# Mixture of experts after selective attention: the singles' first layer turned round, and the last scatters and row fetches placed elsewhere

## The chip, the cores and the metric

The kernel runs on one core of a Trainium2 chip. The metric is the device time of one execution in microseconds (us), the median over several. TensorE multiplies matrices and writes its results to PSUM banks of 128 partitions x 512 float32; ScalarE, VectorE and GpSimd work on them and on SBUF; SyncE and GpSimd issue the transfers (DMA).

## The reference, cut to what matters

```python
# q, k, v: (8, 8, 576, 64), s: (8, 8, 576); x = attention output as (8, 576, 512)
logits = x @ w_gate                         # 8 experts
local_gate = sigmoid(x @ w_local)
for b in range(B):
    for s in range(S):                      # an expert is fresh, or kept from the token before
        e = argmax(logits[b, s]) if s == 0 or local_gate[b, s] < 0.5 else prev_e
        prev_e = e
        h = maximum(x[b, s] @ w1[e], 0)     # w1[e]: 512 x 1024
        out[b, s] = softmax(logits[b, s])[e] * (h @ w2[e])   # w2[e]: 1024 x 512
```

All of it is float32. There are 8 x 576 = 4608 tokens of 512 numbers, and each goes through one expert of two layers. The attention ahead of it is causal, with a bias from a cumulative sum of s.

## The kernel before, in words

**Attention and sorting.** The first third of the time, up to about 255 us, is attention, in 32 steps of one batch and two heads each. As batches are done, groups of them are sorted by expert (class `Group`): `rank` gives each token a slot in a table of rows in memory, `rows_d`, in which each expert has a stretch of its own, and `scatter` writes 128 tokens at a time to their slots by an indirect transfer on GpSimd. A row is 586 numbers (2344 bytes): the token, its number and its gate. The last group, batches 6 and 7, is sorted while the experts' stage already runs, and has ten scatters. After its rank, `Sort.tables` computes on VectorE which expert and which row each later unit of work has, and `Sort.fill` closes each expert's stretch with empty rows, by transfers on SyncE's queue.

**Units of the experts' stage** (`experts`). There are 26 units, in a fixed order: two early ones of 256 rows, whose experts are known beforehand, and then the pattern of `ORDER`, "DDMSSDDMSSDDMSSDDMSSDSDS". D is a double, 256 rows of one expert. S is a single, 128 rows of one expert. M is mixed, 64 rows of each of two experts. There are ten singles. For each unit:

- `load`: the expert's weights w1 and w2, 4 MB, on SyncE's queue, into one of four rooms. The fourth lies in `x4`, the tile that held the tokens of four batches; it is handed to `experts` as `w3`. Of it, the columns from `WS` = 8192 on are not used by weights, and hold `hx`.
- `fetch`: 128 rows at a time from `rows_d`, on GpSimd's queue, behind a read of the row's number from the tables.
- `turn_x`: rows to columns, by VectorE's 32x32 block transposes (L1088), 16 instructions for 128 rows; two small copies (L1104, L1105) keep number and gate.
- `layer1`: for doubles and singles the weights are stationary (128x128) and the turned rows move (256 or 128 columns), so that the result has h already with its hidden index on partitions, as layer 2 wants it (L1231, then an activation on ScalarE, L1235). For mixed units it is the reverse: the rows are stationary, 64 of each expert in one half of the array's columns, and 512 columns of weights move (L1214). Their h comes with rows on partitions, is written to `hx` (L1216), and VectorE turns it into `hT` (L1222, 16 instructions).
- `layer2`: h stationary, 512 columns of w2 moving (L1244); ScalarE multiplies by the gate (L1248, `y`); GpSimd scatters 128 output rows to `out` (L1249).

In the loop, the order written for unit i is: weights of later units, `turn_x(i + 2)`, the first half of `layer1(i + 1)`, `fetch(i + 3)`, the other half, `layer2(i)`. On TensorE therefore the first layer of a unit comes one block before the second layer of the unit ahead of it. Each engine runs its own instructions strictly in the order in which the program writes them.

**Hooks and ticks.** The sorting of the last group is woven into the first units. Matmul groups call `tick()`, and `hooks` lists pairs of a step count and a function; when the count is reached the function's instructions are written at that place in the program. Units 0 and 1 have 16 ticks in each first layer, and 8 in each 128 rows of the second. The ten scatters are one hook at tick 16, the tables eight hooks at ticks 18 to 32, and two final checks stand at 60 and 66.

**The start of the stage** is written out by hand:

```python
        layer1(1, 0, FK)
        load(0)
        fetch(2)
        fetch(3)
        for k in range(2):
            layer2(0, k)
        load(1)
        for k in range(2):
            turn_x(2, k)
        second(1)
```

A fetch of unit 2 or later has to wait until all scatters and fills have landed.

Of the kernel before, what the change touches and what calls it, by code (L numbers as in the profile page):

```python
# [10 lines left out]
F32 = mybir.dt.float32  # L11
# [7 lines left out]
P = 128  # L19
B, H, S, DH = 8, 8, 576, 64  # L20
D = H * DH
E, F = 8, 1024
# [8 lines left out]
DK, FK = D // P, F // P  # L31
# [6 lines left out]
WS = DK * F + FK * D  # L38
XW = XI + 2
R = N + 2 * P  # L40
HALF = P // 2
# [25 lines left out]
@with_exitstack  # L67
def kernel(
    ctx: ExitStack,
    tc: tile.TileContext,  # L70
    q: bass.AP,
    k: bass.AP,
    vm: bass.AP,
    vt: bass.AP,
    kz: bass.AP,
    vz: bass.AP,
    vx: bass.AP,
    s: bass.AP,
    w_gate: bass.AP,
    w_local: bass.AP,  # L80
    w1: bass.AP,
    w2: bass.AP,
    out: bass.AP,
):
    nc = tc.nc
    mm, tr = nc.tensor.matmul, nc.tensor.transpose
    cum_d = nc.dram_tensor("cum", (B * H, S), F32, kind="Internal")
    x_d = nc.dram_tensor("x_tokens", (N, D), F32, kind="Internal")
    rows_d = nc.dram_tensor("x_rows", (E * R + 2 * P, XW), F32, kind="Internal")

    ctx.enter_context(tc.manual_schedule(engines=None))
    const = ctx.enter_context(tc.tile_pool(name="const", bufs=1))
    ident = const.tile([P, P], F32, name="ident")
    make_identity(nc, ident)
    lg = const.tile([P, NM, E + 1], F32, name="lg")
    nc.vector.memset(lg, 0.0)
    recs = const.tile([P, NPAIR, 2 * NB], F32, name="recs")
    nc.vector.memset(recs, 1.0)
    out_of = const.tile([P, 2], I32, name="out_of")
    sort = Sort(tc, const, lg, rows_d, ident, TOPS)  # L100

    with ExitStack() as main:
        keep = main.enter_context(tc.tile_pool(name="keep", bufs=1))
        x4 = keep.tile([P, 4 * NB * XW], F32, name="x4")
        xs = {}

        def new_x(b):
            xs[b] = x4[:, b % 4 * NB * XW : (b % 4 + 1) * NB * XW].rearrange("p (t w) -> p t w", w=XW)
            return xs[b]


        plan = {}

        def at(n, half, *what):
            plan.setdefault((n, half), []).extend(what)

        place = 0
        for bs in ((0, 1), (2, 3), (4,), (5,)):
            n = HP * bs[-1] + HP + 1
            g = sort.group(bs, xs)  # L120
            at(n, 2, g.choose, g.codes)
            at(n + 1, 1, g.rows)
            at(n + 1, 2, g.fresh, g.share, g.held)
            at(n + 2, 1, g.hold)
            at(n + 2, 2, g.hot, g.gates)
            at(n + 3, 1, g.count)
            at(n + 3, 2, g.rank)
            for f in g.scatters:
                place = max(place + (2 if n < 17 else 1), 3 * (n + 4))
                at(place // 3, (3, 4, 0)[place % 3], f)  # L130
        at(3, 0, sort.constants)
        at(26, 2, sort.early)
        gx = main.enter_context(tc.tile_pool(name="gx", bufs=5))
        w = keep.tile([P, WS], F32, name="w0")
        ready = {"w": {0: w}, "x": {}}
        for i in range(8):
            at(14 + i, 0, lambda bank, i=i: load_weights(nc, w, w1, w2, EARLY[0], (i,)))

        def fetch_early(bank):
            for i, e in enumerate(EARLY):  # L140
                for k in range(2):
                    ready["x"][i, k] = gx.tile([P, XW], F32, name="xg")
                    r0 = e * R + k * P
                    nc.sync.dma_start(ready["x"][i, k], rows_d[r0 : r0 + P, :])

        at(27, 1, fetch_early)

        fx = main.enter_context(tc.tile_pool(name="fx", bufs=2))
        turned = ready["turned"] = Turned(nc, fx, main.enter_context(tc.tile_pool(name="first", bufs=2)), ident)
        for j in range(8):  # L150
            at((29, 29, 30, 30, 30, 31, 31, 31)[j], 2,
               lambda bank, j=j: turned.squares(0, j // 4, 2, ready["x"][0, j // 4], (j % 4,)))
        at(31, 2, lambda bank: [turned.extras(0, k, ready["x"].pop((0, k))) for k in range(2)])
        last = sort.group((6, 7), xs)

        attention(tc, q, kz, vz, vx, s, w_gate, w_local, ident, lg, recs, const, new_x, plan)
        tables = sort.tables()
        check = in_range(main.enter_context(tc.tile_pool(name="g_sb", bufs=1)), nc, recs, sort.total, sort.ones, out_of)
        hooks = [(2, last.choose), (2, last.codes), (6, last.rows), (6, last.fresh), (6, last.held), (8, last.share),
                 (11, last.hold), (11, last.hot), (13, last.count), (13, last.rank), (15, last.gates),  # L160
                 (16, lambda bank: [f(bank) for f in last.scatters]),
                 *((18 + 2 * i, lambda bank: next(tables, None)) for i in range(8)),
                 *((60 + 6 * i, lambda bank, f=f: f(bank)) for i, f in enumerate(check))]
        experts(tc, w1, w2, out, rows_d, ident, sort, early_units() + units(), hooks, x4, gx, ready)
    def number(x, most):
        return nc.values_load(x[0:1, 0:1], min_val=0, max_val=most, skip_runtime_bounds_check_because="a count")

    ALL = P * NPAIR * 2 * NB
    with tc.If(number(out_of[:, 1:], ALL + MOST[2]) > 0):
        total = number(sort.total, MOST[2])  # L170
        with tc.If(total > SLOTS[2]):
            experts(tc, w1, w2, out, rows_d, ident, sort, units(SLOTS[2], SLOTS[2] + 4))
            with tc.If(total > SLOTS[2] + 4):
                experts(tc, w1, w2, out, rows_d, ident, sort, units(SLOTS[2] + 4, MOST[2]))
        with tc.If(number(out_of, ALL) > 0):
            general(tc, q, k, vm, vt, s, w_gate, w_local, w1, w2, out, cum_d, x_d, rows_d, ident, lg)
# [876 lines left out]
def early_units():  # L1053
    return [("early", i) for i in range(len(EARLY))]
# [54 lines left out]
def experts(ctx, tc, w1, w2, out, rows_d, ident, sort, units, hooks=(), w3=None, gx=None, ready=None):  # L1109
# [7 lines left out]
    mm, tr = nc.tensor.matmul, nc.tensor.transpose  # L1117
    hooks = list(hooks)
# [10 lines left out]
    fp = pool("fp", 2)  # L1129
# [6 lines left out]
    hT, hx = {}, {}  # L1136
# [59 lines left out]
    def layer1(i, first, last):  # L1196

        if i >= NU:
            return
        n = nbs[i] * P  # L1200
        if first == 0:
            hT[i] = fp.tile([P, FK * 2 * P], F32, name="hT")[:, : FK * n].rearrange("p (f n) -> p f n", f=FK)
        w = [ws[s][:, : DK * F].rearrange("p (c f) -> p c f", c=DK) for s in of[i]]
        if len(w) > 1:

            if first == 0:
                hx[i] = w3[:, WS : WS + F] if ready else fp.tile([P, F], F32, name="hx", bufs=1)
            for g in range(first, last, FK // 2):
                ps = ps_h.tile([P, 512], F32, name="hp")
                f = slice(g * P, g * P + 512)  # L1210
                for c in range(DK):
                    for h in range(2):
                        d = slice(h * HALF, h * HALF + HALF)
                        mm(ps[d], lhsT=xT[i][:, c, d], rhs=w[h][:, c, f], start=(c == 0), stop=(c == DK - 1))  # L1214
                    tick()
                nc.scalar.activation(hx[i][:, f], ps, Act.Relu)  # L1216
            if last == FK:
                x = hx.pop(i).rearrange("p (f n) -> p f n", f=FK)
                m = P // 4
                for a in range(0, P, m):  # L1220
                    for d in range(0, P, m):
                        nc.vector.transpose(hT[i][d : d + m, :, a : a + m], x[a : a + m, :, d : d + m])  # L1222
            return
        per = 512 // n
        for g in range(first, last, per):
            ps = ps_h.tile([P, 512], F32, name="hp")
            for j in range(per):
                f = (g + j) * P
                y = ps[:, j * n : j * n + n]
                for c in range(DK):  # L1230
                    mm(y, lhsT=w[0][:, c, f : f + P], rhs=xT[i][:, c, :], start=(c == 0), stop=(c == DK - 1))  # L1231
                for _ in range(nbs[i]):
                    tick()

            nc.scalar.activation(hT[i][:, g : g + per], ps, Act.Relu)  # L1235
# [34 lines left out]
    if ready:  # L1270
# [4 lines left out]

        layer1(1, 0, FK)
        load(0)
        fetch(2)
        fetch(3)
        for k in range(2):  # L1280
            layer2(0, k)
        load(1)
        for k in range(2):
            turn_x(2, k)
# [73 lines left out]
```

## Time and profile before

| | |
|---|---|
| time before | 790.01 us, median of 3 (788.81 to 790.12) |
| span of the profiled execution | 798.9 us |
| TensorE matmuls | 783.0 us, 98% of the span |
| TensorE weight loads (beside matmuls) | 561.8 us |
| VectorE | 338.4 us |
| ScalarE | 237.0 us |
| GpSimd | 175.4 us |
| moved by DMA | 204.47 MB, mean 256 GB/s |

The profile is one execution, with a record for each instruction: start, duration, and what ended the engine's idle time before it. PE is TensorE's matmuls, PEld its weight loads, DVE VectorE, ACT ScalarE, POOL GpSimd, SP SyncE; a name with a q at its end is the engine's queue. A float32 matmul leaves two records. L1231 is line 1231 of the kernel before. Matmuls overlap, and a record's duration is longer than the step from one start to the next, so a block's length is read from its start to the start of the next block. The profiled execution is some 9 us longer than the timed ones.

### The profile page before, as it was taken

What the parts mean: (1) busy time and instruction counts of PE and PEld (TensorE: products, weight loads), DVE (VectorE), ACT (ScalarE), POOL (GpSimd) and SP (SyncE); (2) the same over time, 40 slices, a digit from 0 to 9 for tenths busy, and PEclk for the clock granted to TensorE, in tenths of its full rate; (3) what the DMA queues carried; (4) which work ended last, traced back from release to release, by engine and by line L of the source; (5) the groups of instructions that cost most, each with busy time, mean ns of one, the idle gap of its engine ahead of it and who ended that gap; (6) DMA issues with size and microseconds to landing.
All of it is one profiled execution on the core that took longest, in us unless ns stands there. A gap on an engine that the chain in (4) does not pass through costs nothing.

```text
span 798.9 us, 18230 instructions
## 1 busy us (share of the span) xinstructions
PE 783.0 (98%) x7078; PEld 561.8 (70%) x7078; DVE 338.4 (42%) x1228; ACT 237.0 (30%) x611; POOL 175.4 (22%) x329
## 2 busy tenths in 40 slices
PE   9999999999999989999999999999999999999996
PEld 8989888888888854853777547774577735676762
DVE  3234444454557649325462264522655226546000
ACT  5767766756664111111111111111111111111110
POOL 3422344455432241101210002101111011011001
PEclk9999999999999999999999999999999999999999
DMA  9485579877474389956999369993699946994001
GB/s 312 170 294 186 187 236 303 312 247 237 170 254 179 113 290 411 393 192 242 335 387 408 127 228 352 387 395 116 246 345 394 361 150 229 373 411 188 22 14 43
DMA packets 64145, 204.47 MB, mean 256 GB/s; under 512 B 8269, under 2 KB 8301, under 8 KB 64048
## 3 DMA queue, kind: packets, MB, share of 16 engines
q1 hardware_dynamic: 55008, 172.41, 60.2%
q0 software_dynamic: 8896, 30.47, 10.0%
q8 instruction: 58, 0.95, 0.5%
q14 instruction: 39, 0.32, 0.1%
q10 hardware_dynamic: 144, 0.33, 0.1%
HBM read 179.93 MB, written 23.76 MB: 255 GB/s over the span
## 4 chain that ended last, share of the span: by engine, by line
issue 59%; PE 30%; POOL 4%; DVE 2%; POOLq 1%; SPq 1%; another core or an unknown queue 1%; DMA 0%; DVEq 0%
PE o L408 13%; PE ps L330 11%; POOL out_dram L1249 2%; PE o L370 2%; POOL xg L1184 2%; PE hp L1231 2%; PE o L286 1%; POOLq L1159 1%; PE o L351 1%; SPq L808 1%; PE bank L947 1%; DVE xT L1088 0%; SPq L804 0%; DVE x L413 0%
## 5 line engine op out<-in xcount | busy, mean ns | idle before, releaser
L1088 DVE STREAM_TRANSPOSE xT<-xg 32x128 f32<-32x128 f32 x576 | 174.2, 302 | 173.3 <-PE hp L1231 97.1
L1244 PE MATMUL yp<-w,hT 128*128 128x512 f32 (+1 forms) x528 | 217.6, 595 | 0.0
L1231 PE MATMUL hp<-xT,w 128*128 128x256 f32 (+1 forms) x1088 | 193.0, 337 | 2.8 <-issue 2.5
L1231 PEld LDWEIGHTS hp<-xT,w 128*128 128x128 f32 x1088 | 172.2, 191 | 27.4 <-issue 11.0
L339 ACT ACTIVATE sc<-ps,bias 128x256 f32<-128x256 f32 (+3 forms) x448 | 156.5, 482 | 60.6 <-PE ps L330 58.6
L1244 PEld LDWEIGHTS yp<-w,hT 128*128 128x128 f32 (+1 forms) x528 | 90.7, 181 | 115.4 <-issue 114.5
L1249 POOL DMA_INDIRECT out_dram<-y,at_gate x38 | 38.5, 1012 | 439.9 <-ACT y L1248 425.4
L408 PE MATMUL o<-v,sc 128*64 128x74 f32 x3072 | 117.9, 229 | 3.1 <-issue 2.9
L408 PEld LDWEIGHTS o<-v,sc 128*64 128x64 f32 x3072 | 110.9, 136 | 11.8 <-issue 9.2
L1235 ACT ACTIVATE hT<-hp 128x512 f32<-128x512 f32 x68 | 40.4, 597 | 195.6 <-PE hp L1231 183.3
L1248 ACT ACTIVATE y<-yp,at_gate 128x512 f32<-128x512 f32 x38 | 26.1, 688 | 240.5 <-PE yp L1244 234.3
L345 POOL TENSOR_SCALAR_AFFINE_SELECT sc<-sc 128x256 f32<-128x256 f32 x160 | 66.5, 420 | 129.0 <-ACT sc L339 60.8
L330 PE MATMUL ps<-q,k 64*128 64x320 f32 (+2 forms) x768 | 92.3, 386 | 0.0
L330 PEld LDWEIGHTS ps<-q,k 64*128 64x128 f32 x768 | 69.6, 186 | 14.6 <-ACT r_v L957 0.6
L1244 PE MATMUL yp<-x,hT 128*128 128x512 f32 (+1 forms) x144 | 63.3, 594 | 0.0
L1222 DVE STREAM_TRANSPOSE hT<-x 32x256 f32<-32x256 f32 x64 | 27.9, 436 | 65.4 <-ACT x L1216 64.5
L410 DVE RECIPROCAL recs<-o 128x4 f32<-128x4 f32 x64 | 12.1, 189 | 92.0 <-PE o L408 80.3
L1231 PEld LDWEIGHTS hp<-xT,x 128*128 128x128 f32 x320 | 46.1, 191 | 5.8 <-issue 2.6
L1231 PE MATMUL hp<-xT,x 128*128 128x128 f32 (+1 forms) x320 | 50.1, 317 | 0.0
L1244 PEld LDWEIGHTS yp<-x,hT 128*128 128x128 f32 (+1 forms) x144 | 25.3, 178 | 26.2 <-issue 25.8
L1038 POOL DMA_INDIRECT x_rows<-x,r_slot_i x40 | 38.9, 973 | 9.3 <-issue 5.7
L413 DVE TENSOR_TENSOR x<-o,recs 128x292 f32<-128x292 f32 x64 | 34.5, 538 | 2.2
(163 smaller groups left out, 350.6 us busy)
## 6 DMA issues: line engine op xcount, KB each, us to landing
w<-in_w_dram SPq DMA_DIRECT2D x184, 512.0 KB
x<-in_w_dram SPq DMA_DIRECT2D x56, 512.0 KB
v<-in_vx_dram SPq DMA_DIRECT2D x32, 370.0 KB
vt<-in_vz_dram SPq DMA_DIRECT2D x32, 320.0 KB
k<-in_kz_dram SPq DMA_DIRECT2D x31, 320.0 KB
q<-in_q_dram SPq DMA_DIRECT2D x32, 288.0 KB
xg<-x_rows POOLq DMA_DIRECT2D x30, 293.0 KB
x_rows<-r_empty SPq DMA_DIRECT2D x6, 293.0 KB
```

The costliest lines, as they stand in the source:

```text
L330: mm(ps[:, h, at : at + z - a], lhsT=kb[d, c * P : c * P + P], rhs=qb[d, a:z], start=True, stop=True)
L339: nc.scalar.activation(scs[n, u][:, h, at : at + z - a], raw[u][:, h, at : at + z - a], Act.Exp, bias=bias[:, i : i + 1], scale=scale)
L345: nc.gpsimd.affine_select(out=x, in_=x, compare_op=Alu.is_ge, fill=0.0, base=0, pattern=[[0, 2], [1, P]], channel_multiplier=-1)
L408: mm(y, lhsT=w, rhs=x, start=start, stop=stop)
L413: nc.vector.tensor_tensor(x, y, rec.unsqueeze(3).to_broadcast([P, t1 - t0, 2, HW]), op=Alu.mult)
L1038: self.s.nc.gpsimd.indirect_dma_start(out=next(self.s.views)[:, :], out_offset=bass.IndirectOffsetOnAxis(ap=self.slot[:z, m : m + 1], axis=0),
L1088: self.nc.vector.transpose(self.xT[i][d : d + m, :, k * P + a * m : k * P + a * m + m], rows[a * m : a * m + m, :, X0 + d : X0 + d + m])
L1222: nc.vector.transpose(hT[i][d : d + m, :, a : a + m], x[a : a + m, :, d : d + m])
L1231: mm(y, lhsT=w[0][:, c, f : f + P], rhs=xT[i][:, c, :], start=(c == 0), stop=(c == DK - 1))
L1235: nc.scalar.activation(hT[i][:, g : g + per], ps, Act.Relu)
L1244: mm(ps[n * m : n * m + m, :], lhsT=hT[i][:, c, a : a + m], rhs=wn[:, c, :], start=(c == 0), stop=(c == FK - 1))
L1249: nc.gpsimd.indirect_dma_start(out=next(outs)[:, :], out_offset=bass.IndirectOffsetOnAxis(ap=at[i, k][:, 0:1], axis=0), in_=y[:, :], eleme ...
```

## The change

There are three edits.

1. Singles take the mixed units' way through layer 1: 128 rows stationary, 512 columns of w1 moving, h written to `hx` by ScalarE and turned by VectorE. The condition is now `nbs[i] == 1`, which holds for singles and mixed units; `m` is 128 rows for one expert and 64 for two. `hx` alternates between two places beside the weights. This is for longer matmuls: 8 of 512 columns instead of 32 of 128.
2. The ten scatters of the last group become ten hooks, at ticks 16, 18, ... 34, and the hooks are sorted by tick. This is to spread them over the program.
3. The fetches of units 2 and 3 are written behind the first block of layer 2, so that the rows behind the scatters are read a block later.

```diff
-                 (16, lambda bank: [f(bank) for f in last.scatters]),
+                 *((16 + 2 * i, f) for i, f in enumerate(last.scatters)),
...
+        hooks.sort(key=lambda hook: hook[0])
...
-        if len(w) > 1:
+        if nbs[i] == 1:
             if first == 0:
-                hx[i] = w3[:, WS : WS + F] if ready else fp.tile([P, F], F32, name="hx", bufs=1)
+                at_ = WS + len(hT) % 2 * F
+                hx[i] = w3[:, at_ : at_ + F] if ready else fp.tile([P, F], F32, name="hx", bufs=1)
+            m = P // len(w)
...
-                    for h in range(2):
-                        d = slice(h * HALF, h * HALF + HALF)
-                        mm(ps[d], lhsT=xT[i][:, c, d], rhs=w[h][:, c, f], start=(c == 0), stop=(c == DK - 1))
+                    for h, wh in enumerate(w):
+                        d = slice(h * m, h * m + m)
+                        mm(ps[d], lhsT=xT[i][:, c, d], rhs=wh[:, c, f], start=(c == 0), stop=(c == DK - 1))
...
         layer1(1, 0, FK)
         load(0)
+        layer2(0, 0)
         fetch(2)
         fetch(3)
-        for k in range(2):
-            layer2(0, k)
+        layer2(0, 1)
```

## The prediction

> **What bounds the kernel now.** I read first the page's shares by engine: TensorE has work nearly all the time. Then TensorE's timeline through the expert stage (from 255 us on), because there the question is what separates one block of matmuls from the next.
>
> ```profile
> PE 783.0 (98%) x7078; PEld 561.8 (70%) x7078; DVE 338.4 (42%) x1228; ACT 237.0 (30%) x611; POOL 175.4 (22%) x329
> ...
> 576.04 7.31 PE L1231 MATMUL hp<-xT,w 128*128 128x128 f32 x64
> 583.28 7.09 PE L1244 MATMUL yp<-w,hT 128*64 128x512 f32 x32
> 590.30 7.41 PE L1231 MATMUL hp<-xT,x 128*128 128x128 f32 x64
> 597.55 7.03 PE L1244 MATMUL yp<-w,hT 128*128 128x512 f32 x16
> 604.42 5.78 PE L1231 MATMUL hp<-xT,w 128*128 128x256 f32 x26
> ```
>
> Columns: start, duration, operation, shapes, count. Every block starts just before the former ends; there is no gap to fill. So this stage lasts as long as TensorE's instructions, and only start-to-start times matter. A single's first layer (64 records of 128 columns) takes 583.28 - 576.04 = 7.24 us; its second layer, with the same arithmetic in 16 records of 512 columns, takes 604.42 - 597.55 = 6.87 us. Third, VectorE's and GpSimd's timelines at the same place, for the slack of what must feed TensorE:
>
> ```profile
> 577.26 0.99 POOL L1249 DMA_INDIRECT out_dram<-y,at_gate  x1 [5.86 <-ACT y L1248]
> 578.22 1.18 POOL L1184 DMA_DIRECT2D xg<-x_rows  x2
> ...
> 587.53 5.04 DVE L1088 STREAM_TRANSPOSE xT<-xg 32x128 f32<-32x128 f32 x16 [12.05 <-DMA xg<-x_rows]
> 592.72 5.04 DVE L1088 STREAM_TRANSPOSE xT<-xg 32x128 f32<-32x128 f32 x16
> ```
>
> The rows of the next double are fetched at 578.22, land at 587.53 (9.3 us later) and are turned by 597.8; TensorE wants them at 604.42, so VectorE has 6.6 us to spare here. Last, the beginning of the stage, where the change also works:
>
> ```profile
> 286.00 0.96 POOL L1038 DMA_INDIRECT x_rows<-x,r_slot_i  x1 [0.30 <-DMA x_rows<-r_empty]
> 292.78 1.20 POOL L1184 DMA_DIRECT2D xg<-x_rows  x2 [5.82 <-issue]
> 294.37 1.14 POOL L1184 DMA_DIRECT2D xg<-x_rows  x2 [0.39 <-issue]
> 299.05 1.04 POOL L1249 DMA_INDIRECT out_dram<-y,at_gate  x1 [3.54 <-ACT y L1248]
> ...
> 299.32 5.04 DVE L1088 STREAM_TRANSPOSE xT<-xg 32x128 f32<-32x128 f32 x16 [2.67 <-DMA xg<-x_rows]
> 304.50 5.03 DVE L1088 STREAM_TRANSPOSE xT<-xg 32x128 f32<-32x128 f32 x16
> ...
> 287.08 0.38 PE L1231 MATMUL hp<-xT,w 128*128 128x256 f32 x1 [1.09 <-issue]
> 288.49 0.40 PE L1231 MATMUL hp<-xT,w 128*128 128x256 f32 x1 [1.03 <-issue]
> 289.23 0.77 PE L1231 MATMUL hp<-xT,w 128*128 128x256 f32 x1 [0.34 <-issue]
> 289.79 28.80 PE L1244 MATMUL yp<-w,hT 128*128 128x512 f32 x64
> 318.42 1.89 PE L1231 MATMUL hp<-xT,w 128*128 128x256 f32 x8
> ```
>
> Two things are seen. TensorE limps at 286 to 289.8 (gaps of 1.09 + 1.03 + 0.34 = 2.46 us) while the ten scatters drain, and the four second-layer blocks after it take 318.42 - 289.79 = 28.63 us instead of 4 x 6.87 = 27.48: the hole costs 3.6 us in all. And the rows of unit 2 are turned by 309.5, 8.9 us before TensorE wants them at 318.42.
>
> **What the skill says.** The Trainium skill, "TensorE: Matmul & The Clock Gate", section "Wait — 56ns, not 53.3ns?", gives a warm start-to-start of N / 2.4 GHz plus about 2.5 ns (55.6 ns at N = 128, 215.7 at 512). The trace agrees if a record is two passes: 7.24 us / 64 = 113 ns = 2 x 56.6, and 6.87 / 16 = 429 ns = 2 x 214.7. So what the new form saves is the fixed cost of 48 records, not arithmetic. "SBUF — State Buffer", section "SBUF: two separate sides", says that VectorE takes the port it shares with GpSimd only in a two-port mode or with two SBUF inputs; the transposes have one. The trace agrees: a fetch issued at 592.49, beside transposes, landed in 8.5 us; the one at 578.22, with VectorE idle, in 9.3. "DMA: Bandwidth & Descriptors", section "Anatomy of one DMA — SWDGE (gpsimd) path", has 2.0 us plus bytes / 436e3, an estimate of 2.7 us for 300 KB of rows; the trace shows 6.5 to 9.3 us beside the weights' traffic, and I use the trace.
>
> **Part 1, the singles' first layer.** Ten singles each drop 32 matmuls (64 records) for 8 (16 records of 512 columns). The ten blocks start to start: 7.24, 7.24, 7.24, 7.25, 7.24, 7.25, 7.24, 7.25, 7.15, 7.14, in all 72.24 us. The two at 7.15 have no half-width block beside them; those at 7.24 do, and about 0.09 of that is the change of form, which may stay. New block: 6.87 us, the second layer's. Saving per single between 7.145 - 6.87 = 0.28 and 7.24 - 6.87 = 0.37; ten give 2.8 to 3.5. I take 3.1. The stage is TensorE's, so all of it shortens the end.
>
> Added on VectorE: 16 transposes of 32x256 per single, as the mixed units have (436 ns each, 7.0 us; 7.20 with gaps), 72 us in all on an engine busy 42%. ScalarE's two activations stay two. What waits: h is needed by layer 2 of the same unit, behind layer 2 of the former unit and layer 1 of the next, at least 13.7 us after its own layer 1; 0.7 us of activation and 7.2 of turning fit. Queued behind these transposes on VectorE is the turning of a later unit's rows. The tightest place is a mixed unit, two singles, then a double, four times. With the times above: layer 1 of the first single ends at 582.9, activation to 583.6, h turned 583.6 to 590.9; the double's rows, landed at 587.53, wait 3.4 us and are turned 590.9 to 601.2. TensorE wants them at 604.42 less two savings of 0.31 = 603.8. Slack 2.6 us: hidden. The second single's h follows, 601.2 to 608.4, wanted at 617.6. The weights are no new limit: the last weights load is issued at about 723, and the block that uses it starts at 764.
>
> **Part 2, the ten scatters spread over ticks 16 to 34.** A tick is a place in program order. What stands between the scatters now is TensorE's matmuls, VectorE's tables and SyncE's fills; nothing of it is GpSimd's, and a scatter waits for slots and gates alone, both ready at 273.8. GpSimd will still issue ten in a row (274.5 to 287.0). I cost it at 0, and the 3.6 us hole stays.
>
> **Part 3, the fetch of units 2 and 3 behind the first layer-2 block.** On GpSimd the fetch now stands behind the first output scatter, which waits for ScalarE's y at 298.8 and ends at 300.09. So it issues at 300.1, not 292.78: 7.3 us later. Its landing: bound below 6.5 us (the present one, no output rows ahead), above 9.3 us (the later fetches, behind an output). I take 8.0, as the output's rows here begin to move sooner after their issue: landed 308.1, both turned 10.2 us later (299.32 to 309.5 now), 318.3 plus about 0.1. TensorE wants them at 318.42. The wait is 0 at the lower bound, 1.3 us at the upper; I take 0.4. Unit 3's turning, behind 1.3 us of checks, ends near 330, before 332.46.
>
> Sum: -3.1 + 0 + 0.4 = -2.7. 790.0 - 2.7 = 787.3 us.
>
> **Rivals.** (a) *The late rows bite harder.* They wait as long as the scatters' hole, over 2 us, and TensorE's clock drops as it did there (0.87 and 0.79 granted at 285 to 295). The skill's clock-gate page, "What's actually happening", says that idleness halves the clock for a window of 3.4 us. A second hole of 3.6 us less the saving: 790.0 - 3.1 + 3.6 = 790.5, no difference to be told. For it: 8.9 us of slack shrink to about zero. Against it: the bounds give at most 1.3 us. (b) *VectorE becomes the limit* at mixed, single, single, double. If its 17.5 us of work there ran 25% longer it would be 4.4 us late against 2.6 of slack, 1.8 us at each of four places: 790.0 - 3.1 + 0.4 + 7.2 = 794.5, slower. Against it: the same transposes show 432 to 442 ns in all 64 cases. (c) *The spread does empty the DMA queues* and the 3.6 us hole goes: 787.3 - 3.6 = 783.7. For it: the hole ends when the scatters have landed. Against it: GpSimd's queue.
>
> **Chances and range.** Forecast 0.70, (a) 0.14, (b) 0.08, (c) 0.08. Within the forecast the saving (2.8 to 3.5) and wait (0 to 1.3) give 786.5 to 788.5, nearly all beyond 0.2% (under 788.4). Faster 0.76, same 0.15, slower 0.09. The range must take in (a)'s milder half and part of what leads to (c): 784.8 to 789.8 leaves out about 0.08 on each side.
>
> **What would show it.** Right: singles' first layer as 16 records at 6.9 us from start to start; VectorE near 410 us busy; ten scatters still back to back on GpSimd and TensorE's gaps before 290 still there; the fetch at about 300; the block at 318.4 waiting for VectorE by under 1.3 us; no TensorE wait on h. Wrong: gaps of TensorE before doubles that follow singles, or a gap-free 280 to 290.

## The result, and the profile after

The changed kernel takes 786.21 us (786.01 to 786.34), the kernel before beside it 789.76: ratio 0.9957, 95% interval 0.9939 to 0.9974, so 2.1 to 4.8 us faster. The forecast was 787.3.

TensorE's timeline of the changed kernel, at the place shown of before (start, duration, operation, shapes, count):

```profile
563.41 7.03 PE L1218 MATMUL hp<-w,xT 128*128 128x512 f32 x16
570.37 7.09 PE L1248 MATMUL yp<-w,hT 128*64 128x512 f32 x32
577.38 7.13 PE L1218 MATMUL hp<-x,xT 128*128 128x512 f32 x16
584.36 7.03 PE L1248 MATMUL yp<-w,hT 128*128 128x512 f32 x16
591.22 13.98 PE L1235 MATMUL hp<-xT,w 128*128 128x256 f32 x64
```

The singles' first layers are 16 records now, and last 6.96 and 6.98 us from start to start, instead of 7.24 and 7.25. No gap stands between the blocks. Over the ten singles: 6.96 four times, 6.98 three times, 6.97 once, and 6.87 twice for the two without a half-width block beside them, in all 69.49 us against 72.24 before: 2.75 us less. The page's first part:

```profile
PE 772.8 (98%) x6598; PEld 516.4 (66%) x6598; DVE 407.4 (52%) x1388; ACT 236.9 (30%) x611; POOL 174.5 (22%) x329
```

VectorE rose by 69 us, which is 160 transposes of 436 ns, and none of it appears in the time. VectorE's timeline, and one line of TensorE's, at the tightest kind of place, a double behind two singles:

```profile
481.33 5.04 DVE L1089 STREAM_TRANSPOSE xT<-xg 32x128 f32<-32x128 f32 x16
...
486.52 5.04 DVE L1089 STREAM_TRANSPOSE xT<-xg 32x128 f32<-32x128 f32 x16
...
491.72 7.17 DVE L1226 STREAM_TRANSPOSE hT<-x 32x256 f32<-32x256 f32 x16
498.92 5.05 DVE L1089 STREAM_TRANSPOSE xT<-xg 32x128 f32<-32x128 f32 x16
...
494.23 13.98 PE L1235 MATMUL hp<-xT,w 128*128 128x256 f32 x64
```

No idle time is noted in brackets: VectorE works without a pause. The double's rows are turned at 491.6; TensorE's block that reads them starts at 494.23. Of the 2.6 us of slack forecast, 2.6 are there.

The start of the stage, in TensorE's, GpSimd's and VectorE's timelines:

```profile
263.85 15.75 PE L1235 MATMUL hp<-xT,w 128*128 128x256 f32 x72
279.43 27.63 PE L1248 MATMUL yp<-w,hT 128*128 128x512 f32 x64
306.90 1.89 PE L1235 MATMUL hp<-xT,w 128*128 128x256 f32 x8
...
267.46 0.93 POOL L1039 DMA_INDIRECT x_rows<-x,r_slot_i  x1 [0.38 <-POOL x L1033]
...
278.76 0.96 POOL L1039 DMA_INDIRECT x_rows<-x,r_slot_i  x1 [0.30 <-issue]
287.52 1.00 POOL L1253 DMA_INDIRECT out_dram<-y,at_gate  x1 [7.80 <-ACT y L1252]
289.20 1.20 POOL L1185 DMA_DIRECT2D xg<-x_rows  x2 [0.68 <-DMA w<-in_w_dram]
...
296.17 5.04 DVE L1089 STREAM_TRANSPOSE xT<-xg 32x128 f32<-32x128 f32 x16 [12.40 <-DMA xg<-x_rows]
301.36 5.03 DVE L1089 STREAM_TRANSPOSE xT<-xg 32x128 f32<-32x128 f32 x16
```

GpSimd still issues the ten scatters in a row, from 267.46 to 278.76, which is 11.3 us from the first start to the last; in the profile before it took 11.5 us (274.51 to 286.00). The ticks have spread them over the program's text and not over time.

The hole ahead of the second layer is gone here, and the rows of unit 2 are turned at 306.4, 0.5 us before they are wanted. It is tempting to book the missing hole as a gain of the spread scatters. The span of this profile is 784.5 us against 798.9 before, 14 us less, where the times differ by 3.5. So the two profiles are not of like executions, and the first experiment is a second profile of the kernel before.

### The profile page after: what moved, and what is told of

Read it like the earlier page. It is cut to its first block, busy times and chain, and to the rows that moved or that the text cites. A ratio compares the mean times of both kernels' runs of the same rounds, so it can differ in the third digit from the quotient of the medians.

```text
span 784.5 us, 17433 instructions
## 1 busy us (share of the span) xinstructions
PE 772.8 (98%) x6598; PEld 516.4 (66%) x6598; DVE 407.4 (52%) x1388; ACT 236.9 (30%) x611; POOL 174.5 (22%) x329
## 4 chain that ended last, share of the span: by engine, by line
issue 55%; PE 34%; POOL 4%; DMA 3%; POOLq 1%; DVE 1%; SPq 0%
PE o L409 14%; PE ps L331 12%; PE hp L1235 4%; PE o L371 2%; POOL out_dram L1253 2%; DMA x<-in_w_dram 2%; POOL xg L1185 2%; DMA w<-in_w_dram 1%; POOLq L1160 1%; PE o L352 1%; DMA s_sb<-in_s_dram 1%; DVE xT L1089 1%; PE bank L948 1%; SPq L1051 0%; PE bank L973 0%
## 5 line engine op out<-in xcount | busy, mean ns | idle before, releaser
L1226 DVE STREAM_TRANSPOSE hT<-x 32x256 f32<-32x256 f32 x224 | 97.6, 436 | 133.1 <-ACT x L1220 130.2
L1235 PE MATMUL hp<-xT,w 128*128 128x256 f32 x640 | 140.7, 379 | 0.3 <-DVE xT L1089 0.3
L1235 PEld LDWEIGHTS hp<-xT,w 128*128 128x128 f32 x640 | 121.1, 190 | 20.2 <-issue 3.8
L409 PE MATMUL o<-v,sc 128*64 128x74 f32 x3072 | 113.6, 229 | 0.7 <-issue 0.7
L409 PEld LDWEIGHTS o<-v,sc 128*64 128x64 f32 x3072 | 108.8, 136 | 8.1 <-issue 6.1
L1218 PE MATMUL hp<-w,xT 128*128 128x512 f32 (+1 forms) x208 | 77.8, 595 | 0.0
L1239 ACT ACTIVATE hT<-hp 128x512 f32<-128x512 f32 x48 | 28.6, 597 | 133.0 <-PE hp L1235 133.0
L1218 PEld LDWEIGHTS hp<-w,xT 128*128 128x128 f32 (+1 forms) x208 | 29.8, 165 | 46.5 <-issue 46.5
L1220 ACT ACTIVATE x<-hp 128x512 f32<-128x512 f32 x28 | 16.7, 597 | 78.8 <-PE hp L1218 78.8
```

Source lines behind the costliest of these rows:

```text
L409: mm(y, lhsT=w, rhs=x, start=start, stop=stop)
L1218: mm(ps[d], lhsT=xT[i][:, c, d], rhs=wh[:, c, f], start=(c == 0), stop=(c == DK - 1))
```

## The experiments

They ran in three sets: e1 to e4 on chip 9, then e5 to e8 on chip 12, then e9 and e10 on chip 9 again. Each ratio is to the kernel before in the same set.

**e1, the kernel before once more.** No edit.

> The kernel before, unchanged, for a second profile of it. Theory A: the hole of TensorE at 286 to 290 us in the first profile (3.6 us) and the 7 us that this profile needed longer for attention than the profile after are of that one execution; a second profile has a span near 788.5, the experts' stage begins near 248, and no hole. Rival B: the hole belongs to the kernel before, and is there again at 3 to 4 us. Ratio to before: 1.000 in both.

Ratio 0.9995 (0.9983 to 1.0007), span 786.7. TensorE's and GpSimd's timelines of this second profile of before:

```profile
263.17 15.74 PE L1231 MATMUL hp<-xT,w 128*128 128x256 f32 x72
278.75 27.63 PE L1244 MATMUL yp<-w,hT 128*128 128x512 f32 x64
306.21 1.89 PE L1231 MATMUL hp<-xT,w 128*128 128x256 f32 x8
...
287.07 1.20 POOL L1184 DMA_DIRECT2D xg<-x_rows  x2 [8.03 <-DMA w<-in_w_dram]
288.68 1.13 POOL L1184 DMA_DIRECT2D xg<-x_rows  x2 [0.40 <-issue]
290.11 1.04 POOL L1249 DMA_INDIRECT out_dram<-y,at_gate  x1 [0.30 <-issue]
```

No hole. This execution took 788.3 us, so those that gave 789.8 us can hardly have had one either. And edit 3 is seen for what it does in this set: in the kernel before the fetch waits until 287.07, and the first output, ready at about 286.6, stands behind it until 290.11; in the changed kernel the output goes at 287.52 and the fetch at 289.20. Counted from the start of the second layer, the fetch comes 1.5 us later (9.77 against 8.32), not 7.3.

**e2, edit 1 alone.** The changed kernel with edits 2 and 3 taken back.

```diff
-                 *((16 + 2 * i, f) for i, f in enumerate(last.scatters)),
+                 (16, lambda bank: [f(bank) for f in last.scatters]),
...
-        layer2(0, 0)
         fetch(2)
         fetch(3)
-        layer2(0, 1)
+        for k in range(2):
+            layer2(0, k)
```

> Edit 1 alone; scatters and fetches as before. Theory A: all of the gain is here: the ten first layers lose 2.75 us (72.24 to 69.49), so the ratio is 0.9965, 787.0 against 789.8, and whatever of the measured 3.55 lies beyond that is the measurement's spread. Rival B: placing the scatters and fetches brought 0.8 us or more: then this kernel stands 0.8 us above the changed kernel in the same call.

785.59 us, ratio 0.9956 (0.9943 to 0.9970). That is the whole change's ratio, 0.9957. All of the gain is edit 1. From the start of unit 2's first layer to the end of the profile, e1 takes 786.7 - 306.21 = 480.5 us and e2 783.3 - 305.64 = 477.7: 2.8 us, the 2.75 counted block by block. The timed gain of 3.5 us does not contradict this: 2.75 us is a ratio of 0.9965, inside both intervals. A few tenths more than 2.75 may be real, and no line of the profile shows them.

**e3, edits 2 and 3 alone.** The kernel before with the two other parts of the change's diff.

> Edits 2 and 3 without edit 1. Theory A: GpSimd issues the scatters in a row as before, and the rows of unit 2 are turned just in time: ratio 1.000, within 0.3 us. Rival B: ratio 0.9985 or less (1.2 us or more faster), with the hole before 290 us gone. Rival C: the late rows cost: TensorE waits 0.5 to 1.3 us ahead of unit 2's first layer, ratio 1.0006 to 1.0016.

788.83 us, ratio 1.0003 (0.9991 to 1.0014). Theory A holds. TensorE's block of unit 2 starts 27.47 us after the first second layer (279.14 to 306.61), as in e1 (27.46). The two edits were not run apart. That the scatters' edit moves nothing is read from the timeline after, where they still go in a row.

**e4, the fetches one block later still.** The changed kernel with this edit.

```diff
-        layer2(0, 0)
+        for k in range(2):
+            layer2(0, k)
         fetch(2)
         fetch(3)
-        layer2(0, 1)
```

> The changed kernel with the fetches of units 2 and 3 behind both layer-2 blocks of unit 0, 6.9 us later again. Theory A: in the changed kernel the rows are turned at 306.4 to 306.5 and wanted at 306.9, so 0.4 us of slack are left; fetched 6.9 us later, TensorE waits about 6.5 us ahead of unit 2, and its clock may drop for a window on top: 6 to 8.5 us slower than the changed kernel, 792 to 795. Rival: the landing is set by the weights' traffic and not by the issue, and less than 3 us are lost.

794.98 us, ratio 1.0079 (1.0064 to 1.0094). Its VectorE and TensorE timelines:

```profile
302.56 5.05 DVE L1089 STREAM_TRANSPOSE xT<-xg 32x128 f32<-32x128 f32 x16 [18.69 <-DMA xg<-x_rows]
307.76 5.04 DVE L1089 STREAM_TRANSPOSE xT<-xg 32x128 f32<-32x128 f32 x16
...
279.64 27.63 PE L1248 MATMUL yp<-w,hT 128*128 128x512 f32 x64
312.89 3.75 PE L1235 MATMUL hp<-xT,w 128*128 128x256 f32 x8 [5.63 <-issue]
...
329.02 13.98 PE L1235 MATMUL hp<-xT,x 128*128 128x256 f32 x64
```

TensorE stands still for 5.6 us, and its next eight records take 3.75 us instead of 1.89: the clock has dropped (0.52 of full speed granted from 310 to 315 us). Unit 3's block starts 49.4 us after the second layer's start instead of 41.5 in the changed kernel, 7.9 us late. The time is 9.4 us above e2's in the same set; the other 1.5 us are there already when the second layer starts (279.64 against 278.18), so they are not this edit's. The changed kernel's half microsecond of slack is real: of the three places tried, its fetch stands at the last one that costs nothing.

**e5 and e6, more work on VectorE.** The changed kernel; of the 16 transposes of each single's h, the first 4 (e5) or 12 (e6) are done twice, to the same place:

```diff
-                        nc.vector.transpose(hT[i][d : d + m, :, a : a + m], x[a : a + m, :, d : d + m])
+                        for _ in range(2 if len(w) == 1 and a < 1 * m else 1):   # e6: 3 * m
+                            nc.vector.transpose(hT[i][d : d + m, :, a : a + m], x[a : a + m, :, d : d + m])
```

> The changed kernel with 4 of the 16 transposes of each single's h done twice: 1.75 us more on VectorE per single. Theory A (slack 2.6 us at the tightest place, turning done 491.6, wanted 494.23): nothing is lost, within 0.3 us of the changed kernel, near 786; the turning of the double's rows ends 0.9 us ahead of TensorE. Rival: VectorE is already at the limit and each of the four places loses most of 1.75 us: 5 to 7 us slower than the changed kernel.

> The changed kernel with 12 of the 16 transposes done twice: 5.25 us more per single. Theory A: the first double's rows come 5.25 - 2.6 = 2.6 us late at each of four places, and the second double's, behind two such singles, 2 to 2.5 us late: 4.5 to 5 us at four places, 18 to 20 us, and up to 8 more where TensorE's clock drops: 804 to 814. Rival: another unit's wait hides it, under 8 us.

e5: 798.63 us, ratio 0.9965 (0.9946 to 0.9984), where the kernel before takes 801.92 in this set: the gain is still whole. In its VectorE and TensorE timelines the double's rows are turned at 504.8 and wanted at 505.61, so 0.8 us of slack is left:

```profile
499.77 5.04 DVE L1089 STREAM_TRANSPOSE xT<-xg 32x128 f32<-32x128 f32 x16
...
505.61 13.98 PE L1236 MATMUL hp<-xT,w 128*128 128x256 f32 x64
```

e6: 820.05 us, ratio 1.0237 (1.0201 to 1.0272), 21.4 us above e5. TensorE's timeline of e6:

```profile
401.01 7.03 PE L1249 MATMUL yp<-w,hT 128*128 128x512 f32 x16
410.94 15.67 PE L1236 MATMUL hp<-xT,w 128*128 128x256 f32 x64 [2.89 <-issue]
426.45 7.03 PE L1249 MATMUL yp<-x,hT 128*128 128x512 f32 x16
434.16 14.05 PE L1236 MATMUL hp<-xT,w 128*128 128x256 f32 x64 [0.68 <-issue]
```

TensorE waits 3 us ahead of the first double, whose block then takes 15.51 us instead of 13.81 on a dropped clock (0.50 granted from 411 to 413 us), and 0.7 us ahead of the second. With the starts compared, that is 5.7 us. The four places lose 5.7, 5.7, 6.2 and 3.1 us, in all 20.7 of the 21.4 timed; at the last one there is no second double in a row, and the clock did not drop. Between 1.75 and 5.25 us more per single, hidden work becomes lost time, as a slack of 2.6 us says.

**e7, one place for hx.** The changed kernel with this edit.

```diff
-                at_ = WS + len(hT) % 2 * F
+                at_ = WS
```

> The changed kernel with one place for hx instead of two in turn. Theory A: the first half of the second single's h is written at about 484, the first single's h has been turned by 481.3: nothing waits, ratio to the changed kernel 1.000. Rival: ScalarE waits for VectorE between the two singles and TensorE for ScalarE's bank: 1 us or more at four places.

799.30 us, ratio 0.9971 (0.9957 to 0.9984), not to be told from e5's 0.9965. The second place does nothing measurable.

**e8, what a record costs.** The kernel before, its singles' first layer cut into moving halves of 64 columns:

```diff
-                for c in range(DK):
-                    mm(y, lhsT=w[0][:, c, f : f + P], rhs=xT[i][:, c, :], start=(c == 0), stop=(c == DK - 1))
+                for r in range(0, n, HALF if nbs[i] == 1 else n):
+                    z = r + HALF if nbs[i] == 1 else n
+                    for c in range(DK):
+                        mm(y[:, r:z], lhsT=w[0][:, c, f : f + P], rhs=xT[i][:, c, r:z], start=(c == 0), stop=(c == DK - 1))
```

> The kernel before with the singles' first layer in moving halves of 64 columns, weights stationary: 128 records per single instead of 64. It measures what a record of this form costs. Theory A, as the prediction put it: a fixed cost of some 6 ns per record on top of its columns (64 columns are 53 ns): 128 x 59.8 = 7.65 us per single, 4 us slower in all, 793. Rival B: at 128 columns the loading of the stationary weights sets the pace (113 ns per record, whatever moves): 128 x 113 = 14.5 us per single, 72 us slower, about 861.

872.67 us, ratio 1.0883 (1.0854 to 1.0911): 70.8 us slower. TensorE's timeline of e8:

```profile
379.73 14.35 PE L1233 MATMUL hp<-xT,w 128*128 128x64 f32 x127
394.01 7.09 PE L1246 MATMUL yp<-w,hT 128*64 128x512 f32 x32
401.02 14.51 PE L1233 MATMUL hp<-xT,x 128*128 128x64 f32 x128
415.37 7.08 PE L1246 MATMUL yp<-w,hT 128*128 128x512 f32 x16
```

A single's first layer has 128 records (the window asked for cut off the first of them at 379.7) and takes 14.3 us. That is 112 ns for a record of 64 columns, and it took 112 to 113 ns for one of 128. From 64 to 128 the moving columns do not matter. e8 alone leaves two readings: a least time for any float32 record, or the load of its stationary 128x128. The profile before decides, in the sorting, where 64 columns move against a stationary of only 2 columns:

```profile
260.82 0.39 PE L947 MATMUL bank<-ident,r_code 128*2 128x64 f32 x4
```

These four records start 55 ns apart (one lasts 0.22 us, so three steps are 0.17). So it is the width of the stationary that sets the 112 ns: each record is paced by its load. The Trainium skill, "TensorE: Matmul & The Clock Gate", section "LDWEIGHTS (loading the stationary operand)", gives P / 1.2 ns for a load of P columns, 107 ns for 128 columns, close to the 112 measured.

**e9 and e10, the whole change and edit 1 alone, on one chip.**

> The changed kernel again, beside edit 1 alone on one chip. Theory A: edits 2 and 3 do nothing to the time: the two stand within 0.1% of each other, both 2.8 to 3.6 us (0.35 to 0.46%) below the kernel before. Rival: edit 3, which lets the first output go 2.6 us earlier and the rows 2 us later, is worth or costs 0.5 us or more.

> Edit 1 alone again, beside the whole change on one chip. Theory A: within 0.1% of it. Rival: 0.5 us or more away from it. Whichever chip it is, if the profile of one kernel of this call has the hole ahead of the first second layer, the other has it as well, since all kernels of the former call had it and none of the call ahead of that.

e9: 800.63 us, ratio 0.9967 (0.9956 to 0.9979). e10: 800.71 us, ratio 0.9961 (0.9947 to 0.9976). The kernel before takes 804.07 here. The two are alike again. Both profiles have the hole; TensorE's timeline of e9, with the scatters spread:

```profile
290.28 0.38 PE L1235 MATMUL hp<-xT,w 128*128 128x256 f32 x1 [1.16 <-issue]
292.41 0.59 PE L1235 MATMUL hp<-xT,w 128*128 128x256 f32 x2 [1.75 <-issue]
292.84 27.63 PE L1248 MATMUL yp<-w,hT 128*128 128x512 f32 x64
320.30 1.89 PE L1235 MATMUL hp<-xT,w 128*128 128x256 f32 x8
```

Every profile of the sets in which the kernel before takes 802 to 804 us has it (e5 to e10, spread scatters or not), none of e1 to e4 has it. It goes with the set, not with the kernel. Nor does it go with the number of the chip: e1 to e4 and e9, e10 all ran on chip 9. In this set edit 3 makes the fetch about as late as forecast, 302.61, which is 9.77 us after the second layer's start against 2.67 in e10, and the rows are still turned 0.5 us before TensorE wants them.

## Why the prediction was right

- **Part 1, the saving.** Forecast 3.1, between 2.8 and 3.5; 2.75 by the blocks, so the lower end. The 0.09 us for the change of form beside half-width blocks did stay: 6.97 there, 6.87 elsewhere.
- **Part 1, its reason.** This step was wrong: "what the new form saves is the fixed cost of 48 records". e8 shows a floor of 112 ns for each record with a 128x128 stationary. Records of 256 and of 512 columns take 216 and 429 ns; a line through both gives 0.83 ns a column and some 2.4 ns besides, so 109 ns at 128 columns, just under the floor (the two singles without a half-width neighbour took 7.14 us / 64 = 111.6). By this estimate 0.12 us of the 0.27 us saved there is the fixed cost, and 0.16 us is the floor. With 512 columns per load the columns set the pace. The sum did not suffer, as it took both blocks' lengths from the trace and not from the reason. At 64 columns the two readings are 67 us apart.
- **Part 1, VectorE.** The slack forecast, 2.6 us, was measured as 2.6, and e5 and e6 bracket it. Rival (b), VectorE as the limit, is real only in e6.
- **Part 2.** Forecast 0; e3 and the pair e9, e10 agree. The scatters go in a row, as forecast. The words that "the 3.6 us hole stays" were wrong for the profile after and for e1, which have none, and right for e5 to e10. A gap-free stretch from 280 to 290 was put down as a sign of being wrong, and the first profile after has it; e1 shows it without any edit, so it speaks neither for nor against. Rival (c) falls with e9: spread scatters, and the hole is there.
- **Part 3.** Forecast a wait of 0.4 us; there is none, and 0.5 us to spare. The rows land 7.0 us after their fetch in both sets (289.20 to 296.17, 302.61 to 309.60), not 8.0, and the fetch goes 9.8 us after the second layer's start, not 10.3. Rival (a) is what e4 shows, one block further.
- **Sum.** Forecast -2.7; -2.75 by the blocks, -3.5 timed. That the sum meets the blocks so closely is luck: the saving was put 0.35 us too high and the wait 0.4 us too high, and the two cancel.

## What to carry to other kernels

Ask which of the two a matmul is paced by, its stationary load or its moving columns: with a 128x128 float32 stationary the load takes about 112 ns per record here, as long as some 130 moving columns. With fewer columns the record still lasts as long as the load (64 columns: twice the time for the same work), and more save little (512 instead of 128: 4% of the block). A turn of the operands that puts 512 columns behind each load may cost a transpose on an idle engine; read that engine's slack at the tightest place, not its busy share. Before a difference between two profiles is put down to an edit, compare their difference in span with that of the times, and profile the unchanged kernel again where they disagree.

## What the runs showed of the hardware

One and the same kernel took 789 us in one set and 802 to 804 in the others, with a mean TensorE clock of 0.99 or more in every profile; in the slower ones the experts' stage runs 7 to 11 us later from its first layers on, and they have the hole at the scatters, in which ScalarE too stands still for 12 us. Chip 9 is named for the set of 789 us and for that of 804, so its number does not explain the difference; what does was not settled.

The length of a stop of TensorE does not tell here whether the clock drops after it. After the 5.6 us of e4 it did (3.75 us for 1.89 us of records). Of the four stops of 2.89 us in e6, three were followed by blocks of 15.5, 15.4 and 16.9 us and the fourth by one of 13.9. After the broken stops at the scatters, 2.3 to 2.5 us in the profile before, e5 and e10, the second layers took 28.6 to 29.2 us; after those of 2.5 to 2.9 us in e6 to e9 they took 27.47, as without a stop. What decides was not tested.
